# The last stage's conversion turns and the first pair's block sums: a change in their order

## The chip, the cores and the metric

The kernel runs on one core of a Trainium2 chip. The metric is the device time of one execution in microseconds; the median of the runs counts.

## What is computed

Three layers stand behind each other on 4 x 576 = 2304 tokens of 512 columns: attention with a block-causal mask, a gated layer whose inputs are mixed with the row before, and a normalised two-layer network that is added to its own input. The change lies in the last one:

```python
def _moe2_ref(x, g_ln, w_ch1, w_ch2) -> np.ndarray:
    mu = np.mean(x, axis=-1, keepdims=True)
    var = np.mean((x - mu) ** 2, axis=-1, keepdims=True)
    xn = (x - mu) / np.sqrt(var + 1e-06) * g_ln
    ch = np.maximum(xn @ w_ch1, 0.0) @ w_ch2
    return (x + ch).astype(np.float32)
```

w_ch1 is 512 x 2048, w_ch2 2048 x 512, all in float32.

## The kernel before

TensorE multiplies in the type fp32r. Each factor is kept as two tiles, a rounded one ("high") and the remainder ("low"), and a product has three passes: high by high, low by high, high by low.

**Chunks and groups.** The last stage cuts the 2048 hidden columns into eight chunks (c = 0 to 7) of 256, and the tokens into five groups of 512, of which number 4 has only 256 tokens: the small group, Z in the code. A chunk takes the groups in the order 0, 3, 4, 2, 1 (chunk 0) or 3, 0, Z, 2, 1 (chunk 1). In chunks 2 to 7 the groups 0 and 3 are a pair, and so are 2 and 1 in some: `em_c1s` makes the first product of a pair with fewer block products, from sums and differences of blocks of the operands. The pair (0, 3) is called P or the first pair, (2, 1) is Q. P and then Z are in chunks 2 to 4 followed by groups 2 and 1 in plain form; in chunks 5 to 7 both pairs take `em_c1s` (Q first in chunk 6), with Z between them.

**The two products.** `em_c1` makes the first product of a group: for each half m of the chunk's 256 hidden columns 12 matmuls into a bank of the pool ph (five banks), then h on ScalarE (relu, rounded) and the remainder of h on VectorE. Between the halves it calls `between()`. The second product, `em_c2`, has 6 matmuls for each block of 128 tokens into a bank of po (three banks); VectorE adds the bank into acc (line 822). The second product of a group is issued one group later, behind the first product of the next.

**Conversion.** The weights of chunk c + 1 are split into high and low while chunk c runs. Per chunk there are four jobs, two for w_ch1 and two for w_ch2, each with the steps load (SP's queue), above and below (exponent pieces, ScalarE), expo (line 130) and bits (line 134) (VectorE), high (rounding, ScalarE) and low (a subtraction, `sub`, line 44). For chunks 0 and 1 low runs on GpSimd; from chunk 2 on it runs on VectorE. The chunks from 2 on have two more kinds of step: forms (four subtractions of weight blocks on VectorE, line 605) and t_high and t_low, which round the forms into the tiles ta or tb (ScalarE) and subtract (VectorE).

**What sets the order.** Every engine works through its instructions in program order. In chunk 0 the conversion of chunk 1 advances in steps at places written out in `first`: one step for x = 1, two for x = 3, four for x = 4, and one more in the first turn of chunk 1. From chunk 1 on there is a list `turns`; each call of `tick()` runs one entry. `group(c, G, todo)` calls it between the halves of the first product, behind it, in the middle of the second product of the group before (unless that group is Z), and behind that.

**The block sums.** `sum_forms` gives four functions f1 to f4 that make the sums of the operand's blocks for a pair, on GpSimd alone, for k = 0 and 1; each ends with a rounding and a subtraction into a tile of SF. f4 writes the tile S3, which until then holds part of group 3's operand. In chunk 0, at x = 4, the kernel opens their temporary tiles and issues f3(0), behind chunk 0 f3(1), and the other six in turns 2 to 7 of chunk 1. The next turns send the four sums to memory (`dma_sums`) and open ta in the place of the temporary tiles (`forms_for`).

Of the kernel before, what the change touches and what calls it, by code (L numbers as in the profile page):

```python
# [32 lines left out]
def attention_moe_kernel(ctx, tc, raw_d, dup_d, raw0_d, dup0_d, v_d, v0_d, msk_d, mz_d, vec_d, eye_d, wk_d, wv_d, wr_d, wc1_d, wc2_d, out_d):  # L33
    nc = tc.nc
# [5 lines left out]
    def act(out, in_, func=AF.Copy, **kw):  # L40
        nc.scalar.activation(out=out, in_=in_, func=func, **kw)  # L41

    def sub(eng, out, in0, in1):
        eng.tensor_tensor(out=out, in0=in0, in1=in1.bitcast(F32), op=ALU.subtract)  # L44
# [102 lines left out]
    def pieces(w, dst, k, n):  # L147

        return [load_split(w[:, f:f + 512], lambda i, f=f: dst(i)[:, k, f:f + 512]) for f in range(0, n, 512)]
# [156 lines left out]
    def tail_z(u):  # L306

        n = len(u[1])
        rs, r3 = [cz.tile([128, 3, 8], F32, name=x)[:, 0:n] for x in ("rsz", "r3z")]

        def q4(x):
            return x.rearrange("p (k s) -> p k s", s=64)

        return [
            lambda x=x: red(out=rs[:, x], in_=v3(SMZ[:, x]), axis=AX.X, op=ALU.max, apply_transpose=True) for x in range(n)
        ] + [lambda: nc.vector.reciprocal(out=r3, in_=rs)] + [
            lambda x=x: nc.vector.transpose(out=v3(RBZ[:, x]), in_=r3[:, x].unsqueeze(2).to_broadcast([128, 8, 32])) for x in range(n)
        ] + [
            lambda x=x, b=b: nc.gpsimd.tensor_tensor(out=XT[b][:, :, 1:65], in0=q4(UZ[:, x]), in1=q4(RBZ[:, x]), op=ALU.mult) for x, b in enumerate(u[1])
        ]  # L320
# [26 lines left out]
    def mm(out, lhsT, rhs, start, stop=True, **kw):  # L347
        nc.tensor.matmul(out=out, lhsT=lhsT, rhs=rhs, start=start, stop=stop, **kw)  # L348
# [238 lines left out]
    def chunk_jobs(c):  # L587
        L, kept = [], []
        for k in (0, 2):
            w = wc1_d[128 * k:128 * k + 256, CF * c:CF * c + CF].rearrange("(a p) n -> p a n", a=2)  # L590
            L.append(load_split(w, lambda i, k=k: W[c % 2][0][i][:, k:k + 2], kept))
        for k in range(2):
            r0 = CF * c + 128 * k
            L += pieces(wc2_d[r0:r0 + 128], lambda i: W[c % 2][1][i], k, DM)
        if c < 2:
            return L
        z = []

        def forms():
            (b11, b12), (b21, b22) = [[st["a2"].rearrange("p (a n) -> p a n", a=2)[:, :, o:o + 128] for o in (0, 128)] for st in kept]  # L600
            raw = stg2.tile([128, 4096], I8, name="raw8")
            z.append(raw.bitcast(F32).rearrange("p (i a n) -> p i a n", i=4, a=2))
            z1, z2, z3, z4 = [z[0][:, i] for i in range(4)]
            for out, in0, in1 in ((z1, b12, b11), (z3, b22, b12), (z2, b22, z1), (z4, b21, z2)):
                tt(out=out, in0=in0, in1=in1, op=ALU.subtract)

        load, above, below, expo, bits, high, low = [list(x) for x in zip(*[(l, a1, a2, x, b, h, w) for l, (a1, a2), (x, b), h, w in L])]
        low = [lambda f=f: f(nc.vector) for f in low]
        t_high, t_low = lambda: act(TF[c][0], z[0]), lambda: sub(nc.vector, TF[c][1], z[0], TF[c][0])
        return [  # L610
            [load[0], load[1]],
            [above[0], below[0]],
            [expo[0], bits[0]],
            [high[0], above[1], below[1], load[2]],
            [expo[1], bits[1]],
            [high[1], above[2], below[2], low[0], load[3]],
            [expo[2], bits[2]],
            [forms, above[3], below[3], high[2]],
            [expo[3], bits[3], t_high],
            [low[1], low[2]],  # L620
            [high[3], t_low],
            [low[3]],
        ]
# [32 lines left out]
    def new_h1(c, G):  # L656
        T["h1", c, G] = h1 = [fn.tile([128, 2, 512], F32R, name=f"h1{i}") for i in range(2)]
        return h1

    def em_c1(c, G, between=lambda: None):  # L660
        n = groups[G][1]
        h1 = new_h1(c, G)
        w1 = W[c % 2][0]
        for m in range(2):
            if m:
                between()
            p = ph.tile([128, 512], F32, name="ph")
            for x, (wi, xi) in enumerate(((0, 0), (1, 0), (0, 1))):
                for kk in range(4):
                    mm(p[:, 0:n], w1[wi][:, kk, 128 * m:128 * m + 128], xn(xi, G, kk), kk == 0 and x == 0, kk == 3 and x == 2)  # L670
            act(h1[0][:, m, 0:n], p[:, 0:n], AF.Relu)
            stt(out=h1[1][:, m, 0:n], in0=p[:, 0:n], scalar=0.0, in1=h1[0][:, m, 0:n].bitcast(F32), op0=ALU.max, op1=ALU.subtract)  # L672
# [9 lines left out]
    def xn(i, G, kk):  # L682
        x, k = XN[G, kk // 2][i]
        return x[:, kk - k]
# [154 lines left out]
    with tc.manual_schedule():  # L839
# [58 lines left out]
        for i in range(N + 2):  # L898
# [54 lines left out]
            if late:  # L953
                take_z(units[i - 2], 2)
                L = tail_z(units[i - 2])
                for a in sorted(set(TAIL_Z)):
                    plan[a] = [f for x, f in zip(TAIL_Z, L) if x == a] + plan.get(a, [])
            if 1 <= i <= N and not mid:
                em_PV(units[i - 1])
                if i == 1:  # L960
                    take_z(units[0], 0)
                    L = tail_z(units[0])
# [162 lines left out]
        def norms(x):  # L1125

            if x + 1 < len(GORD):
                G = GORD[x + 1]
                n = groups[G][1]
                pt = [ph.tile([128, 512], F32, name="ph") for _ in range(4 * n // 512)]  # L1130
                pt = [p[:, o:o + n] for p in pt for o in range(0, 512, n)]
                ln_t(pt, tiles(G))
                ln_out(pt, G)
            if x == 0:
                for i in tiles(GORD[4]):
                    load_acc(i)
            if x + 2 < len(GORD):
                for i in tiles(GORD[x + 2]):
                    ln_z(i, eng=nc.gpsimd if x == 2 else nc.vector)

        Z = GORD[2]
# [6 lines left out]
        for x, G in enumerate(GORD):  # L1148
            em_c1(0, G, lambda: norms(x))
            if x == 0:  # L1150
                ln_scale(late[0], late[-1] + 1)
                conv = Convert(chunk_jobs(1))
            if x == 4:
                es_z.close()
                f1, f2, f3, f4 = open_sums(P)
                f3(0)
            cs = first[x]
            conv.some(cs[0])
            if x:
                em_c2(0, GORD[x - 1], (0, 1))  # L1160
            conv.some(cs[1])
            if x:
                em_c2(0, GORD[x - 1], (2, 3))
            conv.some(cs[2])
        f3(1)
        todo = 0, GORD[-1]
        turns = [[lambda: f1(0)], [lambda: f2(0)], [lambda: f4(0)], [lambda: f1(1)], [lambda: f2(1)], [lambda: f4(1)]]
        turns += [[lambda: dma_sums(P, True, range(4))], [lambda: forms_for(2)]]

        def forms_for(*cc):  # L1170
# [21 lines left out]
        def tick():  # L1192
            if turns:
                for f in turns.pop(0):
                    f()

        def group(c, G, todo):
            c0, G0 = todo
            em_c1(c, G, tick)
            tick()  # L1200
            em_c2(c0, G0, (0, 1))
            if G0 != Z:
                tick()
                em_c2(c0, G0, (2, 3))
            tick()
            return c, G

        for c in range(1, NC2):
            if c + 1 < NC2:
                more = chunk_jobs(c + 1)  # L1210
                if c == 1:
                    turns[0:0] = [[conv.step], []]
                    turns += [[] for _ in range(max(0, 16 - len(turns)))]
                    for x, t in enumerate(more):
                        turns[4 + x] = turns[4 + x] + t
                else:
                    turns += [[] for _ in range(4 * (c < 5))] + more
            if c == 1:
                for G in (P[1], P[0], Z, *Q):
                    todo = group(c, G, todo)  # L1220
                continue
            one, two = (Q, P) if c == 6 else (P, Q)
            em_c1s(c, one, two if c > 4 else None, [lambda ts=ts, x=todo: em_c2(*x, ts) for ts in ((0, 1), (2, 3))], tick)
            if c < 5:
                sums_for(c)
            tick()
            todo = group(c, Z, (c, one[1]))
            if c < 5:
                for G in Q:
                    todo = group(c, G, todo)  # L1230
            else:
                em_c1s(c, two, None, [lambda: em_c2(c, Z, (0, 1))], tick)
                todo = c, two[1]
                tick()
            if c == 4:
                del XN[g3, 0], T["o1"]
                es_o.close()
                TF[6] = tf_tiles(opened(es_f, "fb"), "tb")
# [67 lines left out]
```

## Time and profile before

| what | value |
|---|---|
| median of three runs | 871.43 us (869.27 to 871.61) |
| profiled execution, its own time | 873.15 us |
| its span, first to last instruction | 871.4 us |
| TensorE busy | 810.9 us, 93% |
| VectorE busy | 571.2 us, 66% |
| ScalarE busy | 410.6 us, 47% |
| GpSimd busy | 345.3 us, 40% |
| mean granted clock of TensorE | 0.988 of full speed |

A row of the timeline has the start, the duration from the start of its first instruction to the end of its last, the engine, the line, the operation, out<-in by the program's names, and behind x the number of instructions merged; in square brackets stands the idle time before it and what ended it. PE is TensorE, PEld its weight load, DVE VectorE, ACT ScalarE, POOL GpSimd. TensorE's matmuls overlap, so that starts are compared with starts.

### The profile page before, as it was taken

Reading aid. Unit: us, or ns where it says so; the run is one execution under the profiler, and the core shown is the slowest. Engines: PE = TensorE matmul, PEld = TensorE weight load, DVE = VectorE, ACT = ScalarE, POOL = GpSimd, SP = SyncE. Lnnn points to the kernel's source line nnn. Section 1 sums busy time; section 2 is a strip of 40 time slices with the busy share of each in tenths; the row PEclk is TensorE's granted clock in tenths of the full one; section 3 lists DMA queues with packets and bytes.
Section 4 is the critical chain, followed back from the end, with each engine's and each line's share of the span. In section 5 each row is a group of like instructions: output and inputs, shape, how many; then the busy total and the mean of one; then the engine's idle time right before and its main releaser. Section 6 shows DMA issues by size and latency. Waiting matters only on the chain. (4 is left out here: it accounts for less than half of the span.)

```text
span 871.4 us, 10575 instructions
## 1 busy us (share of the span) xinstructions
PE 810.9 (93%) x3774; PEld 666.7 (77%) x3774; DVE 571.2 (66%) x1018; ACT 410.6 (47%) x707; POOL 345.3 (40%) x307
## 2 busy tenths in 40 slices
PE   3888888889999999999999999898999999999997
PEld 3656666658778998988988888687878788787886
DVE  6899899988784244244287568467475776757544
ACT  5877777778765534535543433133231324334211
POOL 5789679955782011011023489342080531000000
PEclk9999999999999999999999999899999999999999
DMA  8995666613420120002333021604034156151343
GB/s 217 323 326 165 200 212 218 215 64 120 157 74 25 49 72 25 13 37 73 146 124 130 25 72 53 237 25 166 4 103 139 46 196 241 50 206 36 134 155 122
DMA packets 44389, 108.83 MB, mean 125 GB/s; under 512 B 3952, under 2 KB 18416, under 8 KB 42032
## 3 DMA queue, kind: packets, MB, share of 16 engines
q1 hardware_dynamic: 34544, 60.61, 21.2%
q0 software_dynamic: 9360, 45.17, 15.2%
q10 hardware_dynamic: 432, 2.36, 0.7%
q8 instruction: 30, 0.49, 0.2%
q14 instruction: 23, 0.19, 0.1%
HBM read 87.95 MB, written 20.19 MB: 124 GB/s over the span
## 5 line engine op out<-in xcount | busy, mean ns | idle before, releaser
L348 PE MATMUL po<-c,h 128*128 128x512 f32 x864 | 214.2, 399 | 14.9 <-DVE acc L822 10.3
L348 PEld LDWEIGHTS po<-c,h 128*128 128x128 f32 x864 | 162.9, 191 | 56.7 <-DVE acc L822 17.8
L348 PE MATMUL ph<-x,c 128*128 128x512 f32 (+1 forms) x552 | 118.6, 358 | 0.0
L822 DVE TENSOR_TENSOR acc<-po,acc 128x512 f32<-128x512 f32 x144 | 94.8, 685 | 24.0 <-PE po L348 23.2
L348 PEld LDWEIGHTS ph<-x,c 128*128 128x128 f32 x552 | 93.0, 191 | 16.0
L348 PE MATMUL s<-x,wk 128*128 128x384 f32 x576 | 103.1, 338 | 2.2 <-DVE x L44 1.8
L348 PEld LDWEIGHTS s<-x,wk 128*128 128x128 f32 x576 | 101.4, 188 | 3.6 <-DVE x L44 2.1
L44 POOL TENSOR_TENSOR x<-mix,x 128x384 fp32r<-128x384 f32 x36 | 40.4, 1136 | 152.5 <-ACT x L41 149.3
L348 PE MATMUL p<-wv,k 128*128 128x512 f32 x432 | 99.7, 390 | 0.6 <-DVE k L44 0.6
L348 PE MATMUL p<-e,V 128*128 128x512 f32 (+4 forms) x320 | 95.0, 445 | 0.0
L348 PEld LDWEIGHTS p<-wv,k 128*128 128x128 f32 x432 | 80.8, 188 | 17.6 <-DVE k L44 1.0
L348 PEld LDWEIGHTS p<-e,V 128*128 128x128 f32 x320 | 57.7, 194 | 33.9 <-issue 29.0
L44 DVE TENSOR_TENSOR k<-a,k 128x768 fp32r<-128x768 f32 x24 | 23.7, 988 | 81.5 <-ACT a L41 81.5
L41 ACT ACTIVATE h<-ph 128x512 fp32r<-128x512 f32 (+1 forms) x53 | 27.8, 529 | 90.4 <-PE ph L348 90.4
L41 ACT ACTIVATE a<-raw,ce 128x512 f32<-128x512 int8 (+1 forms) x80 | 57.5, 750 | 26.0 <-DVE a L134 20.2
L403 DVE TRANSPOSE_TENSOR_REDUCE part<-s 128x14 f32<-128x448 f32 (+4 forms) x160 | 65.1, 468 | 1.0
L41 ACT ACTIVATE u<-ph 128x512 f32<-128x512 f32 x27 | 16.1, 598 | 93.4 <-PE ph L348 92.0
L672 DVE SCALAR_TENSOR_TENSOR h<-ph,h 128x512 fp32r<-128x512 f32 (+1 forms) x44 | 26.0, 592 | 44.8 <-ACT h L41 44.7
L41 ACT ACTIVATE e<-s 128x1536 f32<-128x1536 f32 (+1 forms) x34 | 48.4, 1424 | 11.8 <-PE s L348 8.9
L348 PE MATMUL s<-wr,x 128*128 128x512 f32 x216 | 51.0, 396 | 2.0 <-DVE x L44 2.0
L348 PE MATMUL s<-QK 128*128 128x512 f32 (+4 forms) x160 | 31.9, 331 | 21.5 <-DVE QK L436 21.2
L740 POOL DMA_DIRECT2D s<-s_scr x12 | 6.4, 537 | 113.9 <-PE ph L348 113.9
(155 smaller groups left out, 1282.5 us busy)
## 6 DMA issues: line engine op xcount, KB each, us to landing
kq<-in_dup_dram POOLq DMA_DIRECT2D x15, 1088.0 KB, 5.9
s<-s_scr POOLq DMA_DIRECT2D x13, 1024.0 KB, 6.7
raw<-in_raw_dram SPq DMA_DIRECT2D x32, 288.0 KB, 4.4
raw<-in_w_ch_dram SPq DMA_DIRECT2D x16, 511.6 KB, 3.6
raw<-in_w_ch_dram SPq DMA_DIRECT2D x32, 255.6 KB, 4.2
V<-in_v_dram SPq DMA_DIRECT2D x16, 320.0 KB, 5.8
s_scr<-s POOLq DMA_DIRECT2D x5, 1024.0 KB, 6.2
x_scr<-r SPq DMA_DIRECT2D x18, 256.0 KB, 2.0
```

Source lines behind the costliest of these rows:

```text
L41: nc.scalar.activation(out=out, in_=in_, func=func, **kw)
L44: eng.tensor_tensor(out=out, in0=in0, in1=in1.bitcast(F32), op=ALU.subtract)
L348: nc.tensor.matmul(out=out, lhsT=lhsT, rhs=rhs, start=start, stop=stop, **kw)
L403: red(out=pt[0:kp, b0:b0 + w // 32, j], in_=v3(s[0:kp, o:o + w]), axis=AX.X, op=ALU.max, apply_transpose=True)
L672: stt(out=h1[1][:, m, 0:n], in0=p[:, 0:n], scalar=0.0, in1=h1[0][:, m, 0:n].bitcast(F32), op0=ALU.max, op1=ALU.subtract)
L740: nc.gpsimd.dma_start(out=SF[i].bitcast(F32), in_=s_scr[PAIRS.index(pr), i])
L822: tt(out=acc[i], in0=p, in1=acc[i], op=ALU.add)
```

## The change

The change has three parts. First, the small group's first product calls no turn between its halves, in any chunk from 1 on. Second, the block sums f3(0) and f3(1) are issued in chunk 0 at x = 3, f1(0) and f2(0) at x = 4, and the other four in turns 2 to 5 of chunk 1; the steps of chunk 2's conversion then begin in turn 3 instead of 4, and the list has 15 entries instead of 16. Third, the low steps of chunk 1's conversion run on VectorE instead of GpSimd. In chunk 1 the first five of chunk 2's turns come one place earlier; the others keep their place relative to the products, since a place has gone. In chunks 2 to 6 the turns from the small group on come one place later.

```diff
@@ -592,6 +592,9 @@
             L += pieces(wc2_d[r0:r0 + 128], lambda i: W[c % 2][1][i], k, DM)
+        if c == 1:
+            for j in L:
+                j[4] = lambda f=j[4]: f(nc.vector)
         if c < 2:
             return L
@@ -1150,10 +1153,14 @@
-            if x == 4:
+            if x == 3:
                 es_z.close()
                 f1, f2, f3, f4 = open_sums(P)
                 f3(0)
+                f3(1)
+            if x == 4:
+                f1(0)
+                f2(0)
             cs = first[x]
@@ -1162,9 +1169,8 @@
-        f3(1)
         todo = 0, GORD[-1]
-        turns = [[lambda: f1(0)], [lambda: f2(0)], [lambda: f4(0)], [lambda: f1(1)], [lambda: f2(1)], [lambda: f4(1)]]
+        turns = [[lambda: f4(0)], [lambda: f1(1)], [lambda: f2(1)], [lambda: f4(1)]]
         turns += [[lambda: dma_sums(P, True, range(4))], [lambda: forms_for(2)]]
@@ -1196,7 +1202,7 @@
         def group(c, G, todo):
             c0, G0 = todo
-            em_c1(c, G, tick)
+            em_c1(c, G, tick if G != Z else lambda: None)
             tick()
@@ -1210,9 +1216,9 @@
                     turns[0:0] = [[conv.step], []]
-                    turns += [[] for _ in range(max(0, 16 - len(turns)))]
+                    turns += [[] for _ in range(15 - len(turns))]
                     for x, t in enumerate(more):
-                        turns[4 + x] = turns[4 + x] + t
+                        turns[3 + x] = turns[3 + x] + t
```

## Rows read from the trace of the kernel before

**Rows 1.** Waits of TensorE, 440 to 872 us: total, times, longest.

```profile
PE po L348 <- DVE acc L822: 10.3, 7, 2.5
PE po L348 <- ACT h L41: 4.0, 1, 4.0
```

**Rows 2.** Timeline of TensorE: products of chunks 2 to 7 beside the small group.

```profile
583.68 4.29 PE L348 MATMUL po<-c,h 128*128 128x512 f32 x18
...
599.05 2.91 PE L348 MATMUL po<-c,h 128*128 128x512 f32 x12
...
636.56 4.28 PE L348 MATMUL po<-c,h 128*128 128x512 f32 x18
...
651.36 2.93 PE L348 MATMUL po<-c,h 128*128 128x512 f32 x12
...
688.98 4.29 PE L348 MATMUL po<-c,h 128*128 128x512 f32 x18
...
702.18 2.91 PE L348 MATMUL po<-c,h 128*128 128x512 f32 x12
...
739.83 4.28 PE L348 MATMUL po<-c,h 128*128 128x512 f32 x18
...
747.14 2.91 PE L348 MATMUL ph<-x,c 128*128 128x512 f32 x12
...
789.08 4.29 PE L348 MATMUL po<-c,h 128*128 128x512 f32 x18
...
796.33 2.90 PE L348 MATMUL ph<-x,c 128*128 128x512 f32 x12
...
837.93 5.64 PE L348 MATMUL po<-c,h 128*128 128x512 f32 x24
843.41 2.93 PE L348 MATMUL ph<-x,c 128*128 128x512 f32 x12
```

**Rows 3.** Timeline of TensorE: the last product of chunk 1, the first of chunk 2.

```profile
546.88 0.40 PE L348 MATMUL po<-c,h 128*128 128x512 f32 x1
551.24 8.80 PE L348 MATMUL po<-c,h 128*128 128x512 f32 x23 [3.96 <-ACT h L41]
559.87 2.90 PE L348 MATMUL ph<-x,c 128*128 128x512 f32 x12
```

**Rows 4.** Windows: busy PE, PEld, DVE, ACT, POOL, then clock, DMA share, GB/s.

```profile
551.00:557.00 6.00, 5.73 (x13) 4.05 (x14) 5.79 (x9) 1.68 (x4) 0.78 (x2) 0.50 1.02 414
```

**Rows 5.** Timeline of ScalarE: the rounding of the forms in chunk 1.

```profile
549.64 1.06 ACT L41 ACTIVATE ta<-raw 128x1024 fp32r<-128x1024 f32 x1 [10.31 <-POOL s L44]
```

**Rows 6.** Timeline of GpSimd: the start of the first pair's sums.

```profile
484.92 2.62 POOL L696 TENSOR_TENSOR t<-x,s 128x512 f32<-128x512 f32 x2 [4.06 <-PE ph L645]
```

**Rows 7.** Waits of GpSimd, 490 to 508 us.

```profile
POOL c L44 <- ACT c L41: 12.3, 3, 6.4
```

**Rows 8.** Timeline of VectorE: the small group in chunk 2.

```profile
586.17 0.43 DVE L672 SCALAR_TENSOR_TENSOR h<-ph,h 128x256 fp32r<-128x256 f32 x1 [1.93 <-ACT h L41]
586.51 1.66 DVE L130 TENSOR_TENSOR a<-a,a 128x512 int32<-128x512 f32 x1
```

**Rows 9.** Timeline of VectorE: chunk 0's end, chunk 1's conversion.

```profile
497.40 1.81 DVE L130 TENSOR_TENSOR a<-a,a 128x512 int32<-128x512 f32 x1
...
499.91 1.28 DVE L822 TENSOR_TENSOR acc<-po,acc 128x512 f32<-128x512 f32 x2
501.47 0.69 DVE L130 TENSOR_TENSOR a<-a,a 128x512 int32<-128x512 f32 x1 [0.27 <-ACT a L41]
...
503.81 1.28 DVE L822 TENSOR_TENSOR acc<-po,acc 128x512 f32<-128x512 f32 x2
```

**Rows 10.** Line 44 on VectorE, 508 to 800 us: durations in ns, min/median/max.

```profile
L44 DVE TENSOR_TENSOR c<-a,c x23: 681/684/1837, 530.2 to 795.9; 128x512 fp32r<-128x512 f32 x23
L44 DVE TENSOR_TENSOR ta<-raw,ta x5: 1216/1217/1218, 554.2 to 797.7; 128x1024 fp32r<-128x1024 f32 x5
```

**Rows 11.** Timeline of TensorE's weight loads in chunk 1's first product.

```profile
503.39 0.32 PEld L348 LDWEIGHTS ph<-x,c 128*128 128x128 f32 x2
```

## The prediction

> **What bounds the kernel now.** I read the table of waits of TensorE in the last stage first, since the page has TensorE busy for 93% of the span and everything the change touches lies in that stage. It names two things only [rows 1]: seven waits for the additions into acc on VectorE, 10.3 us together and 2.5 us at the longest, and one wait of 4.0 us for an h of ScalarE. The timeline of TensorE then gives their places.
>
> The h wait stands at the end of chunk 1, before the second product of group 2. That product has 24 matmuls of 512 columns; the same work without a wait, in chunk 7, goes from 837.93 to 843.41, 5.48 us [rows 2]. Here it goes from 546.88 to 559.87, 12.99 us [rows 3], so 7.51 us are lost. Only some 4 us of that is the wait; behind it TensorE's granted clock is 0.50, which is 1.2 GHz, from 551 to 557 [rows 4], and half of those 6 us is 3.0 us. Who was late is seen on ScalarE: the rounding of the forms (ta) stood 10.3 us at the head of its queue and waited for GpSimd's last block sum of the first pair, until 549.64 [rows 5]; the h that TensorE wanted stood behind it. So GpSimd bounds this place. Its sums begin at 484.92 [rows 6], and then the queue stands idle three times for 12.3 us, because subtractions of chunk 1's conversion lie between the sums and wait for ScalarE [rows 7].
>
> The waits for acc stand in the second product beside the small group, in chunks 2 to 6. From the start of that product to the start of the next one that is not in question, chunks 2, 3 and 4 take 15.37, 14.80 and 13.20 us for 48 matmuls (two times 5.48, 10.96), and chunks 5 and 6 take 7.31 and 7.25 us for 24 [rows 2]. The losses are 4.41, 3.84, 2.24, 1.83 and 1.77: 14.09 us, idle time and slower clock together. Their cause is read on VectorE in chunk 2: it does nothing for 1.93 us until ScalarE has the second h of the small group, and straight behind come the next conversion instructions, the first of 1.66 us [rows 8], and only then the additions that free a bank of po. ScalarE is late with that h since the turn between the two halves of the first product put a rounding and two exponent pieces in front of it.
>
> **The small group's turn.** With no turn between the halves, ScalarE makes both h one behind the other, as soon as TensorE has the products, and the turn runs after the second. In chunks 2 to 4 that turn holds work for ScalarE and a load alone, so VectorE goes from the second h to the first addition; the exponent and bit steps come a place later, behind two additions. Three banks of po mean that the fourth block waits for the first addition, 18 matmuls or 4.11 us after the product starts. The addition can end about 2 us after it (the first block takes a quarter of 5.48, and an addition 0.64, half of 1.28 [rows 9]). In chunks 5 and 6 the forms' four subtractions over 256 columns stand ahead of it: an estimated 0.4 us each, from 0.68 for 512 columns [rows 10], and 2.0 + 1.6 = 3.6 is still ahead of 4.11. So I take all 14.09 as gained. The moved steps' loads leave one to three us later, while SP's queue holds only loads; what waits for them is ScalarE's exponent work one product later, and the 5.5 us of that product cover it. Without that cover a late load costs its own few us once per chunk.
>
> What is late next in chunks 2 to 4 is the forms' subtraction, 1.22 us [rows 10], which comes to stand between the last h of group 1 and the first addition behind it. With three passes of about 0.7 us (h on ScalarE, its remainder on VectorE, the addition) and the 1.22, that addition ends near 3.4 us after its product's start, against 4.11: 0.7 us of cover, so I count nothing.
>
> **The sums of the first pair.** The same instructions, begun earlier in GpSimd's queue and with no subtraction of chunk 1 between them: they end the 12.3 us sooner, 549.6 - 12.3 = 537.3 at the latest. TensorE would need the rounding of ta to start by 546.88 - (551.24 - 549.64) = 545.3. So there are 8 us to spare and the 7.51 us go. The four transfers of the sums to memory leave earlier too, beside the last weight load of chunk 2; the h behind that load is wanted only after two further products, some 8 us, which hide it.
>
> **The four subtractions of chunk 1 go to VectorE, and this costs.** The second has to be there before chunk 1's first product can use the low weights. TensorE loaded those at 503.39, already at the moment when GpSimd had finished [rows 11]. On VectorE it comes behind the additions of the product before. By the rows of this place [rows 9]: additions until 501.19, the first subtraction, the next exponent and bit pair 2.34 (501.47 to 503.81), two additions 1.28, the second subtraction. One subtraction takes 0.68 to 1.84 on VectorE [rows 10]; I take the middle, 1.26. 501.19 + 1.26 + 2.34 + 1.28 + 1.26 = 507.33, so TensorE waits 3.9 us where it did not. Bounds: 1.38 for the pair and 0.68 for each subtraction give 1.8; 1.81 for each of the four [rows 9], and 1.1 for an earlier pair pushed on too, give 7.2. On top comes the clock: the nearest row is the 4.0 us wait, 3.0 us; the least is none, since chunks 4 to 6 lose about 2 us each, hardly more than a wait of that size itself. I take 3.0, together 6.9, bounds 1.8 to 10.2.
>
> VectorE's subtractions of one size take 0.68 us or up to 1.84 [rows 10], so something else holds the long ones up. The Trainium skill, SBUF — State Buffer, section Who interferes with whom, says that a VectorE instruction with two SBUF inputs and a GpSimd instruction that reads SBUF exclude each other, and that the later one is blocked for the whole of the other. That speaks against this edit, because the subtractions move to VectorE just where GpSimd no longer pauses; by that rule all of them would be long ones, and the trace agrees as far as 1.84 us goes.
>
> **The sum.** 14.09 + 7.51 - 6.9 = 14.7 us. Against the profiled execution, 873.15 us (span 871.4), that is 858.4; it is 1.7 us above the median of the runs, so against the median, 871.43, I forecast 856.7. With the bounds of the loss, 851.4 to 860.
>
> **Rivals.**
> *The subtractions are in time.* If VectorE's pairs shrink to 1.38 and the additions come sooner, TensorE loses next to nothing: 871.43 - 21.6 = 849.8. Against it, the long instructions in [rows 9] stand beside only a few GpSimd ones, and there will be more.
> *Every instruction waits for a whole one.* Six VectorE instructions with two SBUF inputs, from 497.40 to the second subtraction, each wait for one of GpSimd's 1.31 us (half of 2.62 [rows 6]) and then take 0.68: 11.9 us and 2.6 for the additions end at 511.9, 8.5 us after 503.39. With the clock: 871.43 - 21.6 + 11.5 = 861.3. The rule of the Trainium skill named above, SBUF — State Buffer, leads to this time if no instruction escapes it. Against it, most such instructions in the rows are shorter.
> *The wait comes back in group 1.* If VectorE is more than 0.7 us behind when it comes to the forms' subtraction, chunks 2 to 4 lose there what they gained: 856.7 + 10.5 = 867.2.
> *GpSimd is not sooner.* If the fourth sum, which writes where chunk 1's first product reads, or more VectorE work beside it, holds the queue up by 8 us, the 7.51 stay: 864.2.
> *The change does not do what it says:* the acc waits have another cause and stay, and chunk 1 gains 7.5 and loses 6.9: 870.8.
> *Slower.* Starving of VectorE ahead of chunk 1's first product. To end 0.3% above the median it must cost 24.2 us, thus 21.2 of waiting beside the 3.0 of clock, 2.9 us more for each of the six instructions than in my sum, about 4 us each. The longest in the rows is 1.84. Slower than 874.0.
>
> **How the numbers follow.** Forecast 0.58, its own range 851.4 to 860; in time 0.12; a whole instruction each 0.08; back in group 1 0.08; GpSimd not sooner 0.07; no effect 0.04; slower 0.03. About 0.3% (2.6 us) is what a measurement of this kernel can tell from no change. Faster is all but the last two, 0.93; same 0.04; slower 0.03. To leave out no more than 2 in 10 the range reaches to the case in time and to GpSimd not sooner: 849 to 865.
>
> **What would show it.** Right: no wait for acc in chunks 2 to 6, ta's rounding waiting for nothing on GpSimd, 5.5 us for the product at the end of chunk 1, and a new wait of 2 to 7 us in chunk 1's first product for a subtraction on VectorE, with a clock of 0.5 behind it. Wrong: an acc wait in group 1's product, GpSimd's last sum of the first pair after 545, or a first product of chunk 1 without a wait.

## The result and the profile after

The changed kernel takes 858.47 us (median; 857.15 to 858.88), the kernel before, timed beside it, 871.52 us. The ratio is 0.985, 95% interval 0.982 to 0.988, a gain of 13 us. The profiled execution took 857.15 us with a span of 855.1; before it was 871.4, so between the two profiles 16.3 us have to be accounted for. In the changed code the lines of [rows 1 to 11] behind L595 stand 3 further down (L822 is now L825); some of the experiments below keep the old numbers.

TensorE's waits in the last stage, kernel after (total, times, longest), which answer to [rows 1]:

```profile
PE ph L348 <- DVE c L44: 3.8, 1, 3.8
PE po L348 <- DVE acc L825: 0.9, 2, 0.5
```

Of the seven waits for acc the five beside the small group in chunks 2 to 6 (9.5 us together) are gone, and so is the 4.0 us for an h; of the two short ones that are left one was there before, at the end of chunk 0, and one is new. One new wait of 3.8 us has come, for a subtraction on VectorE. TensorE's timeline gives the places (start, duration; in brackets idle time and releaser):

```profile
501.98 0.62 PE L348 MATMUL ph<-s,c 128*128 128x512 f32 x2
...
502.89 0.62 PE L348 MATMUL ph<-s,c 128*128 128x512 f32 x2
507.31 0.74 PE L348 MATMUL ph<-x,c 128*128 128x512 f32 x2 [3.79 <-DVE c L44]
...
513.16 5.66 PE L348 MATMUL po<-c,h 128*128 128x512 f32 x24
518.65 5.66 PE L348 MATMUL ph<-x,c 128*128 128x512 f32 x24
...
528.84 1.66 PE L348 MATMUL po<-c,h 128*128 128x512 f32 x6 [0.41 <-DVE acc L825]
...
552.44 5.65 PE L348 MATMUL po<-c,h 128*128 128x512 f32 x24
557.92 2.92 PE L348 MATMUL ph<-x,c 128*128 128x512 f32 x12
...
581.76 5.65 PE L348 MATMUL po<-c,h 128*128 128x512 f32 x24
587.25 5.62 PE L348 MATMUL ph<-x,c 128*128 128x512 f32 x24
592.71 2.91 PE L348 MATMUL po<-c,h 128*128 128x512 f32 x12
...
630.25 5.64 PE L348 MATMUL po<-c,h 128*128 128x512 f32 x24
...
678.85 5.66 PE L348 MATMUL po<-c,h 128*128 128x512 f32 x24
...
727.47 5.63 PE L348 MATMUL po<-c,h 128*128 128x512 f32 x24
...
774.89 5.65 PE L348 MATMUL po<-c,h 128*128 128x512 f32 x24
```

Against [rows 2]: in chunk 2 the stretch that took 15.37 us now goes from 581.76 to 592.71, 10.95, so 4.42 are won there. Chunks 3 to 6 (the last four rows, to 641.24, 689.81, 732.93 and 780.39) take 10.99, 10.96, 5.46 and 5.50 us by the same reading, where they took 14.80, 13.20, 7.31 and 7.25. All five together give 14.07 us. Against [rows 3]: the product at the end of chunk 1 goes from 552.44 to 557.92, 5.48 us where it was 12.99; that gives 7.51. Lost is time in chunk 1's first product, from 501.98 to 513.16, 11.18 us, while 24 such matmuls without a wait, the ones behind it, take 5.49. Of these 5.69 us, 3.96 are the wait (the pair due at 502.89 + 0.46 = 503.35 began at 507.31), and the other 1.73 the clock behind it. This window (busy PE, PEld, DVE, ACT, POOL, then clock, DMA share, GB/s) answers to [rows 4]; the windows of 3 us on either side of it have 0.97 and 0.96:

```profile
509.00:512.00 3.00, 3.00 (x8) 2.33 (x8) 3.00 (x3) 1.12 (x2) 2.92 (x3) 0.50 0.24 66
```

VectorE shows who was late (compare [rows 9]), and GpSimd what it had beside it (compare [rows 6]):

```profile
500.95 0.68 DVE L44 TENSOR_TENSOR c<-a,c 128x512 fp32r<-128x512 f32 x1
501.55 1.78 DVE L130 TENSOR_TENSOR a<-a,a 128x512 int32<-128x512 f32 x1
503.42 0.93 DVE L134 SCALAR_TENSOR_TENSOR a<-raw,a 128x512 int32<-128x512 int32 x1
504.27 1.28 DVE L825 TENSOR_TENSOR acc<-po,acc 128x512 f32<-128x512 f32 x2
505.47 1.78 DVE L44 TENSOR_TENSOR c<-a,c 128x512 fp32r<-128x512 f32 x1
```

```profile
501.07 1.71 POOL L699 TENSOR_TENSOR t<-t 128x512 f32<-128x512 f32 x1
502.87 0.94 POOL L706 TENSOR_SCALAR s<-t 128x512 fp32r<-128x512 f32 x1
503.89 1.58 POOL L44 TENSOR_TENSOR s<-t,s 128x512 fp32r<-128x512 f32 x1
505.43 2.96 POOL L699 TENSOR_TENSOR t<-t,x 128x512 f32<-128x512 f32 x2
...
531.52 1.61 POOL L44 TENSOR_TENSOR s<-t,s 128x512 fp32r<-128x512 f32 x1
```

GpSimd goes through its sums without a pause and ends them at 533.1 instead of 549.6. The subtraction that the low weights wait for is the last one of VectorE's five, to 507.25. ScalarE's rounding of the forms, [rows 5], waits for nothing now:

```profile
542.13 1.05 ACT L41 ACTIVATE ta<-raw 128x1024 fp32r<-128x1024 f32 x1
```

The account between the profiles: 14.07 + 7.51 - 5.69 = 15.89. Small items follow that the prediction did not count. Chunk 1 has a wait for acc in the product ahead of its small group (524.14 to 530.34 with the wait at 528.84, against 5.48: 0.72 lost) and had one in the product behind it (526.92 to 533.13 before: 0.73 won). The last product of chunk 0 begins 0.28 us sooner and takes 0.1 more. That makes 16.1 of 16.3. The medians differ by 13.05 us only: the profiled execution after lies 1.3 us below its median and the one before 1.6 above its own.

### The profile page after: what moved, and what is told of

Same layout as the page of the kernel before. It is cut to its first block, busy times and chain, and to the rows that moved or that the text cites. A ratio compares the mean times of both kernels' runs of the same rounds, so it can differ in the third digit from the quotient of the medians.

```text
span 855.1 us, 10569 instructions
## 1 busy us (share of the span) xinstructions
PE 804.5 (94%) x3774; PEld 663.5 (78%) x3774; DVE 569.6 (67%) x1022; ACT 411.4 (48%) x707; POOL 341.7 (40%) x303
## 5 line engine op out<-in xcount | busy, mean ns | idle before, releaser
L348 PE MATMUL po<-c,h 128*128 128x512 f32 x864 | 208.2, 393 | 1.5 <-DVE acc L825 0.9
L348 PEld LDWEIGHTS po<-c,h 128*128 128x128 f32 x864 | 160.9, 188 | 39.8 <-DVE acc L825 5.5
L825 DVE TENSOR_TENSOR acc<-po,acc 128x512 f32<-128x512 f32 x144 | 95.1, 685 | 27.4 <-PE po L348 26.4
L41 ACT ACTIVATE a<-raw,ce 128x512 f32<-128x512 int8 (+1 forms) x80 | 57.5, 752 | 25.3 <-DVE a L134 16.9
L41 ACT ACTIVATE u<-ph 128x512 f32<-128x512 f32 x27 | 16.1, 598 | 87.5 <-PE ph L348 86.2
L348 PE MATMUL s<-wr,x 128*128 128x512 f32 x216 | 52.9, 405 | 3.0 <-DVE x L44 3.0
L348 PEld LDWEIGHTS s<-wr,x 128*128 128x128 f32 x216 | 41.4, 193 | 14.1 <-DVE x L44 4.3
L41 ACT ACTIVATE a<-s 128x768 f32<-128x768 f32 x24 | 19.5, 812 | 67.6 <-PE s L348 63.4
```

The source lines that it names most:

```text
L825: tt(out=acc[i], in0=p, in1=acc[i], op=ALU.add)
```

## The experiments

Theory: the gain comes from the small group's turn alone; sums and subtractions together win 7.5 us at the end of chunk 1 and pay nearly as much at its start, because VectorE is held up by GpSimd's sums. The rivals are told with the runs. All ratios are against the kernel before, with 95% intervals.

**One part at a time.** First only the turn between the halves taken out, on the kernel before:

```
-            em_c1(c, G, tick)
+            em_c1(c, G, tick if G != Z else lambda: None)
```

> Only the first part of the change: no turn between the halves of the small group's product. Theory (three separate terms: 14.1 us from the small group in chunks 2 to 6, 7.5 us at the end of chunk 1 from the sums, a loss of 5.7 us in chunk 1's first product from the subtractions on VectorE): 871.5 - 14.1 - 0.6 (chunk 1's small group) = 856.8 us, between 855 and 859; no wait for acc beside the small group. At the end of chunk 1 the rounding of ta now lies behind the second h of group 2, so the wait there becomes one for an addition, some 5 us and a slower clock, a loss of 5 to 8 in place of 7.5. No wait in chunk 1's first product. Rival (the small group's gain needs a GpSimd that is done earlier): the acc waits of chunks 2 to 4 stay in part, over 862.

Then the change without this line:

```
-            em_c1(c, G, tick if G != Z else lambda: None)
+            em_c1(c, G, tick)
```

> The change with the turn between the halves of the small group's product kept: the sums early and the subtractions on VectorE alone. Theory of three terms: 871.5 - 7.5 + 5.8 = 869.8, between 868 and 871.5; acc waits beside the small group in chunks 2 to 6 as before, 9.5 us together; the new wait of 3.8 us for a subtraction in chunk 1's first product. Rival (the two edits of chunk 0 and 1 are worth more than their difference, since a quiet GpSimd also shortens later waits): under 867.

The turn alone: 859.12 us, ratio 0.985 (0.983 to 0.987), the same as the whole change. The two other parts alone: 872.38 us, ratio 1.000 (0.998 to 1.002), nothing. The first is 0.1 us above the expected range, the second 2.6 above the expected time and 0.9 above its range; the kernel before, timed beside both, took 872.96 us, not the 871.5 from which both were worked out. TensorE's waits without the turn, and then with it kept:

```profile
PE po L348 <- DVE acc L822: 5.5, 2, 5.1
```

```profile
PE po L348 <- DVE acc L825: 11.3, 8, 2.5
PE ph L348 <- DVE c L44: 3.8, 1, 3.8
```

Without the turn the acc waits of chunks 2 to 6 are gone, and 5.1 us of wait at the end of chunk 1 remain (12.10 us from 546.26 to 558.36, a loss of 6.6). With it kept they are all there, the end of chunk 1 is free, and the 3.8 us at its start are new. So the gains add up, and the two other edits together cancel out.

**Which of the two makes GpSimd early?** The change, with the sums issued where they stood before, and the subtractions on VectorE:

```
-            if x == 3:
+            if x == 4:
...
-                f3(1)
-            if x == 4:
-                f1(0)
-                f2(0)
...
+        f3(1)
...
-        turns = [[lambda: f4(0)], [lambda: f1(1)], [lambda: f2(1)], [lambda: f4(1)]]
+        turns = [[lambda: f1(0)], [lambda: f2(0)], [lambda: f4(0)], [lambda: f1(1)], [lambda: f2(1)], [lambda: f4(1)]]
```

With the sums, the steps of chunk 2's conversion go back to where they were: they begin in turn 4, and the list has 16 entries.

> The small group without a turn and chunk 1's subtractions on VectorE, but the block sums issued in their old places. Theory: what held GpSimd up were the subtractions between the sums, not the place in the program; without them GpSimd runs its sums from 484.6 on without a pause wherever they are issued. So the last sum ends before 537, ta waits for nothing on GpSimd, and the time is that of the changed kernel, 858.5 (857 to 860). Rival (the earlier places in the program bring the gain): the last sum ends after 545 and the time is 865 to 866.

857.87 us, ratio 0.983 (0.982 to 0.985), the same time as the change. GpSimd's last sum of the pair:

```profile
531.84 1.30 POOL L44 TENSOR_TENSOR s<-t,s 128x512 fp32r<-128x512 f32 x1
```

It ends at the same moment as in the change (533.1). Once the subtractions have left GpSimd's queue, the place of the sums in the program is therefore worth nothing: nothing that waits for ScalarE stands between them any more.

Then the other half: sums early, but the subtractions left on GpSimd.

```
-        if c == 1:
-            for j in L:
-                j[4] = lambda f=j[4]: f(nc.vector)
```

> The change with chunk 1's subtractions left on GpSimd, behind the sums that were moved ahead of them. Theory: the second subtraction then ends after both f3, f1(0) and f2(0) and the first subtraction, near 513.5 instead of 507.3, so the wait in chunk 1's first product is 10 us, the clock at half for some 6 us behind it, and the time 858.5 + 6 to 8 = 865 to 867. Rival (VectorE is no better a place than GpSimd, since the two hold each other up): within 2 us of the changed kernel.

862.97 us, ratio 0.989 (0.988 to 0.991), 2 us below the expected range. TensorE and GpSimd at the start of chunk 1:

```profile
512.49 1.22 PE L348 MATMUL ph<-s,c 128*128 128x512 f32 x2 [7.90 <-POOL c L44]
```

```profile
509.96 1.26 POOL L44 TENSOR_TENSOR s<-t,s 128x512 fp32r<-128x512 f32 x1
511.18 2.51 POOL L44 TENSOR_TENSOR c<-a,c 128x512 fp32r<-128x512 f32 x2
```

The subtractions stand behind the early sums; TensorE waits 7.9 us instead of 3.8. I had expected 10. On VectorE they are thus worth 4.5 us once the sums are early. The end of chunk 1, however, is free here too. GpSimd's last sum and TensorE's product there:

```profile
537.62 1.62 POOL L44 TENSOR_TENSOR s<-t,s 128x512 fp32r<-128x512 f32 x1
```

```profile
558.52 5.65 PE L348 MATMUL po<-c,h 128*128 128x512 f32 x24
```

Behind the early sums the subtractions hold GpSimd up for 1.5 us instead of 12.3, and its last sum ends at 539.2. TensorE runs 6 us behind the change here, but 539.2 is also ahead of the 545.3 at which the prediction wanted the rounding of ta. So either edit to GpSimd's queue is enough to free the end of chunk 1: the subtractions taken out, or the sums put ahead of them.

**What makes VectorE late at the start of chunk 1?** By the theory GpSimd's sums beside it, by the rival the length of its own queue. In the next kernel GpSimd makes f3(0) and then a one-column copy that reads an h of chunk 1's first group, so that it stands still while VectorE converts (the expectation speaks of four block sums ahead of the copy; the edit leaves this one):

```
+    held = cst.tile([128, 1], F32, name="held")
...
-                f3(1)
-            if x == 4:
-                f1(0)
-                f2(0)
...
-        turns = [[lambda: f4(0)], [lambda: f1(1)], [lambda: f2(1)], [lambda: f4(1)]]
+        turns = [[lambda: hold_pool(), lambda: f3(1), lambda: f1(0), lambda: f2(0), lambda: f4(0)], [lambda: f1(1)], [lambda: f2(1)], [lambda: f4(1)]]
...
+        def hold_pool():
+            nc.gpsimd.tensor_copy(out=held, in_=T["h1", 1, P[1]][1][:, 1, 0:1].bitcast(F32))
```

> The changed kernel, with one difference: behind the first four block sums GpSimd makes a one-column copy that reads an h of chunk 1's first group, so that it stands still while VectorE converts chunk 1's last weights; the other sums of the first pair follow behind that copy. Nothing of the computation is left out. Theory (GpSimd's sums are what stretches VectorE's instructions there): both subtractions, the exponent and the bit step take about 0.7 us each; 500.95 + 0.68 + 1.38 + 1.28 + 0.68 = 504.97, so TensorE, ready at 503.52, waits about 1.4 us (1 to 2) in chunk 1's first product, and the granted clock behind it stays above 0.9. Rival (the queue of VectorE alone, whatever GpSimd does): the wait stays at 3.5 to 4 us. The held sums end near 547 to 550, so the loss at the end of chunk 1 comes back to about 5 to 7 us and the time as a whole stays near that of the changed kernel, 857 to 863.

GpSimd stood still from 491.0 to 510.0. VectorE, and the one wait of TensorE in that product (lines from 59 on stand one further down here):

```profile
500.19 0.68 DVE L44 TENSOR_TENSOR c<-a,c 128x512 fp32r<-128x512 f32 x1
500.79 0.69 DVE L131 TENSOR_TENSOR a<-a,a 128x512 int32<-128x512 f32 x1
501.56 0.69 DVE L135 SCALAR_TENSOR_TENSOR a<-raw,a 128x512 int32<-128x512 int32 x1
502.17 1.28 DVE L826 TENSOR_TENSOR acc<-po,acc 128x512 f32<-128x512 f32 x2
503.37 0.68 DVE L44 TENSOR_TENSOR c<-a,c 128x512 fp32r<-128x512 f32 x1
```

```profile
504.11 0.73 PE L349 MATMUL ph<-x,c 128*128 128x512 f32 x2 [0.78 <-DVE c L44]
```

Every instruction takes 0.68 or 0.69 us, the same five end after 3.86 us instead of 6.30, the wait is 0.78 us, below the expected range, and the granted clock stays at 1.00 from 494 to 515. So the sums beside them account for 3.0 of the 3.8 us and for the lower clock; the queue's own length is the other 0.8. As expected the sums then end late (550.8) and the end of chunk 1 loses 7.45 us. The time, 863.99 us from one execution alone, is 1 us above the expected range. Of its span 2.7 us were lost behind the end of chunk 1, where it does the same work as the change with matmuls a few ns longer; why is open.

**Can chunk 1's conversion be put elsewhere?** One step of it a place earlier, on the change:

```
-        first = (0, 0, 0), (0, 0, 1), (0, 0, 0), (0, 1, 1), (1, 1, 2)
+        first = (0, 0, 0), (0, 0, 1), (0, 0, 1), (0, 1, 1), (1, 1, 1)
```

> The changed kernel with one of the seven conversion steps of chunk 0 moved from x = 4 to x = 2, so that at x = 4 the second subtraction stands ahead of the last two additions instead of behind them. Theory (the wait in chunk 1's first product is VectorE's queue: a pair, two additions and a subtraction too many ahead of it): the second subtraction ends near 503.7, TensorE wants it near 504.6, no wait and no slower clock; the fourth block at x = 4 waits some 1.3 us more for its bank. 858.5 - 5.7 + 1.3 = 854.1 us (853 to 856). Rival (the wait follows GpSimd's sums, whose reads hold the subtraction up wherever it stands): the wait of 3.8 us stays and the time is within 1.5 us of 858.5.

859.51 us, ratio 0.985 (0.983 to 0.987): no gain, a miss. The time is that of the rival, but not its wait: no subtraction is waited for. TensorE's only long wait, and VectorE ahead of it:

```profile
506.26 2.93 PE L348 MATMUL po<-c,h 128*128 128x512 f32 x6 [6.03 <-DVE acc L825]
```

```profile
500.56 1.29 DVE L675 SCALAR_TENSOR_TENSOR h<-ph,h 128x512 fp32r<-128x512 f32 x2 [1.96 <-ACT h L41]
501.76 1.15 DVE L44 TENSOR_TENSOR c<-a,c 128x512 fp32r<-128x512 f32 x1
502.84 1.09 DVE L130 TENSOR_TENSOR a<-a,a 128x512 int32<-128x512 f32 x1
504.02 1.58 DVE L134 SCALAR_TENSOR_TENSOR a<-raw,a 128x512 int32<-128x512 int32 x1
505.52 1.27 DVE L825 TENSOR_TENSOR acc<-po,acc 128x512 f32<-128x512 f32 x2
```

The wait moved. Now three conversion instructions stand between the h and the first addition, with two exponent pieces ahead of the h on ScalarE, and TensorE waits 6.0 us for a free bank. Two steps earlier, each at a place with room:

```
-        first = (0, 0, 0), (0, 0, 1), (0, 0, 0), (0, 1, 1), (1, 1, 2)
+        first = (0, 0, 0), (0, 0, 1), (0, 1, 1), (0, 1, 1), (0, 1, 1)
```

> The changed kernel with the conversion of chunk 1 two steps further on before x = 4, so that the second subtraction comes right behind the first two additions there. Theory: no wait for a subtraction in chunk 1's first product and no further wait at x = 4: 858.5 - 5.7 = 852.8 us (851.5 to 855), unless the exponent work at x = 2 and 3, beside the normalisation, makes an addition late there by 1 us or so. Rival as for the run with one step: within 1.5 us of 858.5.

854.88 us, ratio 0.980 (0.978 to 0.982). That is within the range expected. No subtraction is waited for; 1.93 us for acc remain at 502.77.

**Is the late h the cause of the acc waits?** The prediction said that the turn makes ScalarE's second h late. In this kernel the turn stays between the halves, and the one behind them is dropped, so the h stays late and the next conversion instructions don't stand ahead of the additions:

```
-            em_c1(c, G, tick if G != Z else lambda: None)
-            tick()
+            em_c1(c, G, tick)
+            if G != Z:
+                tick()
```

> The changed kernel, but in the small group the turn stays between the halves of the first product and the one behind the product goes. The number and order of the turns are the same; only this one place differs. Theory of the prediction (ScalarE is late with the second h since the turn's rounding and exponent pieces stand in front of it, and the conversion then stands ahead of the additions): both halves matter, but the first addition has about 0.5 us to spare in chunks 2 to 4 once no exponent and bit steps stand in front of it, so 858.5 + 0 to 2. Rival (the late h alone is the cause): the waits of 2 us in chunks 2 to 4 come back, 864 or more.

861.10 us, ratio 0.987 (0.985 to 0.989), 0.6 us above the expected range. Its span is 4.3 us longer than that of the change; 2 us of that it lost ahead of chunk 1 (the last product of chunk 0 begins at 497.73, there at 495.68) and 1.1 in chunk 1's first product, where the clock stayed low for longer (last section). In chunk 2, which answers to [rows 8], VectorE and TensorE:

```profile
587.68 0.42 DVE L675 SCALAR_TENSOR_TENSOR h<-ph,h 128x256 fp32r<-128x256 f32 x1 [1.93 <-ACT h L41]
588.02 1.28 DVE L825 TENSOR_TENSOR acc<-po,acc 128x512 f32<-128x512 f32 x2
```

```profile
585.19 5.66 PE L348 MATMUL po<-c,h 128*128 128x512 f32 x24
590.68 5.62 PE L348 MATMUL ph<-x,c 128*128 128x512 f32 x24
```

The h is as late as before: VectorE stands idle for 1.93 us and has it 2.49 us behind the start of TensorE's product in both (587.68 and 585.19; 586.17 and 583.68 before). Yet TensorE does not wait; of the five waits in chunks 2 to 6 one of 0.2 us is left, in chunk 5. The late h alone doesn't make the wait; it takes the exponent and bit steps between it and the first addition. Whether these alone would do it was not tried.

**The same gain at the end of chunk 1 without moving any sum.** On the kernel before, the turn out, and chunk 2's conversion begun three turns later:

```
-            em_c1(c, G, tick)
+            em_c1(c, G, tick if G != Z else lambda: None)
...
-                    turns += [[] for _ in range(max(0, 16 - len(turns)))]
-                    for x, t in enumerate(more):
-                        turns[4 + x] = turns[4 + x] + t
+                    turns += [[] for _ in range(19 - len(turns))]
+                    (expo3, bits3, t_high), (low1, low2), (high3, t_low), (low3,) = more[8:]
+                    for x, t in enumerate(more[:8] + [[t_high, low1], [expo3, bits3], [high3, t_low], [low2, low3]]):
+                        turns[7 + x] = turns[7 + x] + t
...
-                    turns += [[] for _ in range(4 * (c < 5))] + more
+                    turns += [[] for _ in range(4 * (c < 5) - len(turns))] + more
```

The last pair of lines takes the turns that run over into chunk 2 off the empty ones there.

> The kernel before with the small group's turn taken out, the sums and the subtractions of chunk 1 left on GpSimd where they were, and instead chunk 2's conversion begun three turns later in chunk 1, so that the rounding of ta comes behind the last h of group 1 (its subtraction in the last turn, the two last low steps in chunk 2's first turn). Theory: GpSimd still ends at 549 to 550, but nothing that TensorE waits for stands behind ta in ScalarE's queue, so the 7.5 us at the end of chunk 1 go and the 5.7 us in its first product never come: 872 - 14.1 - 7.5 = 850 us (849 to 853). Rival (ta is needed so soon in chunk 2 that the wait only moves to its third block product): 855 or more.

852.54 us, ratio 0.977 (0.976 to 0.979), within the range expected, and better than both kernels. GpSimd's last sum and ScalarE there:

```profile
548.41 1.34 POOL L44 TENSOR_TENSOR s<-t,s 128x512 fp32r<-128x512 f32 x1
```

```profile
549.87 0.58 ACT L41 ACTIVATE h<-ph 128x512 fp32r<-128x512 f32 x1
550.59 1.06 ACT L41 ACTIVATE ta<-raw 128x1024 fp32r<-128x1024 f32 x1
```

The sums end at 549.7, as late as in the kernel before, and it costs 1.2 us only (547.26 to 553.92, against 5.48): the h that TensorE wants is now ahead of the rounding in ScalarE's queue. Nothing had to be made early, and the start of chunk 1 pays nothing.

The same with the turn kept (the first two lines of the diff undone):

> The version with chunk 2's conversion begun three turns later, but with the turn between the halves of the small group's product kept. If the two gains add, the waits for acc in chunks 2 to 6 come back with their 14.1 us and the end of chunk 1 stays near 6.7 us: 852.5 + 14.1 = 866.6 (865 to 868). Rival (a gain of the later conversion needs the missing turn, since the forms' rounding stands behind it): the 6 to 7 us at the end of chunk 1 come back too, 872 to 873.

869.19 us, ratio 0.997 (0.995 to 0.999), between the two expectations. The acc waits of chunks 2 to 6 are back, and the end of chunk 1 loses 4.0 us instead of 1.2 (548.76 to 558.24). Here an h still stands behind the rounding of ta in ScalarE's queue (552.24 behind 551.27), where the version without the turn has none. So at this place the later conversion wins 3.5 of 7.5 us while the turn is kept, and 5.4 of 6.6 without it; the two spans, 868.3 and 851.4, are 16.9 apart: 14.1 + 2.8.

## Why the prediction was right, and where not

- **The forecast** of 856.7 us was 1.8 below the median; of the cases told, the likeliest came. Its own measure was the profile, where it gave 858.4 against 857.15: 1.25 us too slow, which is about the clock term below. That the forecast against the median came out too low instead lies in which executions were profiled, one 1.6 us above its median before and one 1.3 below after.
- **The small group's turn, 14.09 us:** 14.07. Taken chunk by chunk it holds within 0.03 us. The first experiment shows it alone. What stood behind it in the argument, 0.7 us of cover for the first addition behind the forms' subtraction, held: no acc wait there. The reading of [rows 1] was loose: two of the seven waits, of 0.4 us each, stand ahead of chunk 2, and the 14.09 us don't hold them.
- **Its cause** was told in two links, ScalarE's late h and the conversion instructions behind it. The run with the same late h and no wait shows that the first link doesn't suffice. The sum was right since the change takes out both.
- **The end of chunk 1, 7.51 us:** 7.51. But the step "begun earlier in GpSimd's queue and with no subtraction of chunk 1 between them" named two causes as if both were needed, and either is enough: issued late without the subtractions, the sums end at 533.1 as in the change; issued early with the subtractions behind them, they end at 539.2, and that product takes 5.5 us too. And the claim "GpSimd bounds this place" was half the truth: the version with the later conversion and no turn has the same late sums and loses 1.2 us. What bound it was the order of ScalarE's queue.
- **The loss at the start of chunk 1, 6.9 us:** 5.69. The wait was sized well, 3.9 against 3.96, the second subtraction to end at 507.33 against 507.25, though by other parts: I took 1.26 for each subtraction and 2.34 for the pair, and they took 0.68, 1.78 and 2.8 (501.55 to 504.35). That their errors cancel to 0.1 us is luck. The mis-sized term is the clock, 3.0 us taken from [rows 4] and 1.73 measured. Two sums of the bounds are off by 0.2: the terms of the upper one give 7.4 us, not 7.2, and 1.8 us of loss gives 851.6, not 851.4.
- **A new wait for acc in chunk 1,** 0.72 us, was not seen, and is made good by the one that went.
- **Sums and subtractions together** were 7.51 - 6.9 = +0.6 us by the prediction; measured alone they give a ratio of 1.000. It said so without drawing the conclusion, that these edits were not needed.
- **The rival "every instruction waits for a whole one"**, 861.3, did not come about. The Trainium skill, SBUF — State Buffer, section Who interferes with whom, has a VectorE instruction with two SBUF inputs contend with a GpSimd one that reads SBUF for an exclusive lock. The rows agree: 0.68 us with GpSimd still, up to 1.78 with it at work. What the rival had too large is the wait of each. In the rows shown after the change, VectorE's exponent step ends 0.55 us behind the end of the GpSimd instruction that was running when it began (503.33 and 502.78), and the bit step 0.54 us behind (504.35 and 503.81). So each waits for the rest of an instruction and not for a whole one of 1.31 us, and the first subtraction, which began when GpSimd was all but done (500.95, and 500.99 on GpSimd), took 0.68.

## What to carry to other kernels

In this kernel an engine's late result cost only what stood behind it in the queues: look first which instruction waits at the head of a queue, and whether what TensorE wants stands behind it; to put the waiting one later can be worth more than to make its data early. Put the work that frees a buffer (here the additions that free a bank of po) directly behind what it depends on, and filler behind that. And time each part of a change alone: here one line brought all of it, and the two others cancelled out.

## What was not expected of the hardware

- The clock behind a wait is not in proportion to the wait: behind 3.96 us [rows 3] it was 0.50 for 6 us [rows 4], behind 3.79 us for about 3.4 us (matmul pairs of 0.85 us instead of 0.46, 508.81 to 512.19). To take the row of the nearest wait as its price was off by 1.3 us. Nor is it the same behind the same wait: in the version that drops the turn behind the product, the pairs stayed that slow from 509.36 to 515.41, and chunk 1's first product lost 2.87 us to the clock instead of 1.73. So the 3.0 us could as well have come true; what decides it is open.

```profile
509.36 1.22 PE L348 MATMUL ph<-x,c 128*128 128x512 f32 x2 [3.80 <-DVE c L44]
...
514.64 0.94 PE L348 MATMUL ph<-x,c 128*128 128x512 f32 x2
```

- GpSimd is lengthened in turn: its 1.30 us instructions (531.84 above) took 1.58 to 1.71 us beside VectorE's work (501.07, 503.89).
